# Chunked attention feeding a multiplicative FFN: transposes moved from DMA to 64x64 quadrants of the matrix engine

## Chip, core and metric

The kernel runs on one core of one Trainium2 chip. The metric is the device time of one execution in microseconds (us). Before the change it is about 313 us. A few runs are in a second, slower state (one of the four before, 318.63 us, is one): medians are over all runs, ratios over the fast ones alone. In a call of several kernels, all are timed in rounds beside the kernel before on the same chip. The engines are PE (matrix), DVE (vector), ACT (scalar), POOL (here, after setting up constants, it only issues loads), and SP (here it only issues DMAs).

## Reference

```python
# q, k, v: (8 batches, 8 heads, 576 tokens, 64); chunks of 64 tokens attend only to themselves
scores = 1/8 * q_c @ k_c.T          # per head and chunk, 64x64
attn   = softmax(scores)
x      = (attn @ v_c), heads side by side   # (4608 tokens, 512)
a = x @ w1; b = x @ w2              # 512 -> 1024
out = ((a * b) @ w3) @ w_out        # 1024 -> 1024 -> 512
```

The kernel multiplies w3 by w_out first (w3o), works in bfloat16, and walks over 36 units of 128 tokens (two chunks). In the kernel's matmuls the dimension that is summed over lies on partitions, so PE needs q and k with the head dimension on partitions, and x with its 512 features on partitions. What comes from memory, and what the value product gives, has tokens on partitions. Hence the transposes that this study is about: 8 blocks of 128x128 per unit for q and k, 4 for x.

## The kernel before

Loads are issued by POOL, which also casts float32 to bfloat16 on the way. After the first four units (the head, where PE transposes), every transpose is a DMA from SBUF to SBUF, issued by SP:

```python
def load(dst, src):
    return inorder(nc.gpsimd.dma_start(dst, src))
def turn(dst, src):
    return inorder(nc.sync.dma_start_transpose(dst, src))

def turn_qk(b, g0, g1):              # several 128x512 groups of one batch at a time
    turn(qkT_tile(b)[:, g0:g1]..., qk_t[b][:, g0:g1, :]...)
def turn_x(u):
    turn(xt[:, :, u * UT:(u + 1) * UT], xn_t.pop(u))

def do_S(u):    # 16 matmuls of 64x64, one per head and chunk, spread over four quadrants of the array; exp on ACT
def do_PV(u):   # 16 matmuls of 64x65 (the 65th column sums the weights); reciprocal, product on DVE -> xn
def PV_step(u):
    do_PV(u)
    turn_x(u)
# [cut] steady part, for each of four steps n of a tile t of 512 tokens:
place(0, lambda u=u: S_step(u + 1)); place(0, lambda u=u: PV_step(u))
do_ab(t, 2 * n); do_ab(t, 2 * n + 1); do_o(t - 1, n)
```

The softmax here doesn't subtract the row's maximum and nothing guards it: scores larger than these inputs give would overflow.

Of the kernel before, what the change touches and what calls it, by code (L numbers as in the profile page):

```python
# [11 lines left out]
def kernel(  # L12
# [54 lines left out]
    def turn(dst, src):  # L67

        return inorder(nc.sync.dma_start_transpose(dst, src))  # L69

# [14 lines left out]
    NP = S // UT  # L85
    G = 2 * NP + 1
    qk_t, qkT_t = {}, {}

    def rows(src, b, t0, n):
        return src[b, :, t0:t0 + n, :].rearrange("h p d -> p h d")  # L90

    def load_qk(b, i):
        if b not in qk_t:
            qk_t[b] = io.tile([P, G, DM], bf, tag="qk", bufs=3, name="qk")
        if i < NP:
            for t, src in enumerate((q, k)):
                load(qk_t[b][:, 2 * i + t, :].rearrange("p (h d) -> p h d", d=D),
                     rows(src, b, i * UT, UT))
        else:
            for p0, src in ((0, q), (CH, k)):  # L100
                load(qk_t[b][p0:p0 + CH, 2 * NP, :].rearrange("p (h d) -> p h d", d=D),
                     rows(src, b, NP * UT, CH))

    def load_batch(b):
        for i in range(NP + 1):
            load_qk(b, i)
# [9 lines left out]
    def qkT_tile(b):  # L116
        if b not in qkT_t:
            qkT_t[b] = io.tile([P, G, NHP, P], bf, tag="qkT", name="qkT")
        return qkT_t[b]

    def turn_qk(b, g0, g1):
        turn(qkT_tile(b)[:, g0:g1].rearrange("p g n t -> p (g n) t"),
             qk_t[b][:, g0:g1, :].rearrange("p g m -> p (g m)"))

    def pe_turn_qk(b, g):

        tp = ps.tile([P, NHP, P], bf, tag="m", bufs=4, name="qktp")
        for n in range(NHP):
            tr(tp[:, n, :], qk_t[b][:, g, n * P:(n + 1) * P], ident[:])
        nc.vector.tensor_copy(qkT_tile(b)[:, g], tp[:])  # L130

    def at(b, c, n, isk):
        i, o = divmod(c, 2)
        if i < NP:
            return qkT_t[b][:, 2 * i + isk, n, o * CH:(o + 1) * CH]
        return qkT_t[b][:, 2 * NP, n, isk * CH:(isk + 1) * CH]
# [3 lines left out]
    def chunk_at(u, ci):  # L140
        return divmod(2 * u + ci, NCH)

    NM = NHP // 2
    e_t, xn_t = {}, {}

    def do_S(u):
        sp = ps.tile([P, 2, 512], f32, tag="s", name="sp")
        sv = sp[:, :, 0:NHP * CH].rearrange("p r (m c q) -> p r m c q", m=NM, c=2)
        for ci in range(2):
            b, c = chunk_at(u, ci)  # L150
            for m in range(NM):
                for t in range(2):
                    for r in range(2):
                        h = slice(r * CH, (r + 1) * CH)
                        mm(sv[t * CH:(t + 1) * CH, r, m, ci, :],
                           lhsT=at(b, c, 2 * t + m, 1)[h], rhs=at(b, c, 2 * t + m, 0)[h],
                           start=True, stop=True)
        e = asb.tile([P, 2, NM, 2, CH], bf, tag="e", name="e")
        nc.scalar.activation(e[:].rearrange("p r m c q -> p r (m c q)"), sp[:, :, 0:NHP * CH],  # L159
                             Exp, scale=scale, bias=0.0)  # L160
        e_t[u] = e

    def do_PV(u):
        xp = ps.tile([P, 2, 512], f32, tag="x", name="xp")
        e = e_t.pop(u)
        W = D + 1
        for m in range(NM):
            for r in range(2):
                for ci in range(2):
                    b, c = chunk_at(u, ci)  # L170
                    for t in range(2):
                        h = slice(t * CH, (t + 1) * CH)
                        n = 2 * m + r
                        mm(xp[ci * CH:(ci + 1) * CH, t, n * W:(n + 1) * W],
                           lhsT=e[h, r, m, ci, :], rhs=vbuf[b % NV][h, n, c, 0:W],
                           start=True, stop=True)
        xv = xp[:, :, 0:NHP * W].rearrange("p t (n w) -> p t n w", w=W)
        rc = asb.tile([P, 2, NHP, 1], f32, tag="rc", name="rc")
        nc.vector.reciprocal(rc[:], xv[:, :, :, D:D + 1])  # L179
        xn = asb.tile([P, 2, NHP, D], bf, tag="xn", bufs=3, name="xn")  # L180
        nc.vector.tensor_mul(xn[:], xv[:, :, :, 0:D], rc.to_broadcast([P, 2, NHP, D]))  # L181
        xn_t[u] = xn[:].rearrange("p t n d -> p (t n d)")

    def turn_x(u):
        turn(xt[:, :, u * UT:(u + 1) * UT], xn_t.pop(u))

    def pe_turn_x(u):
        xn = xn_t.pop(u)
        tp = ps.tile([P, NHP, P], bf, tag="m", bufs=4, name="xtp")
        for n in range(NHP):  # L190
            tr(tp[:, n, :], xn[:, n * P:(n + 1) * P], ident[:])
        nc.vector.tensor_copy(xt[:, :, u * UT:(u + 1) * UT], tp[:])
# [12 lines left out]
    def do_a(t, j, tag="a_sb", bufs=2):  # L205
        n = tiles[t][1]
        a_ps = ps.tile([P, TT], f32, tag="m", bufs=4, name="a_ps")
        mm_ab(w1, a_ps, t, j)
        a_t[j] = msb.tile([P, TT], f32, tag=tag, bufs=bufs, name="a_sb")
        nc.scalar.copy(a_t[j][:, 0:n], a_ps[:, 0:n])  # L210
# [13 lines left out]
    def do_o(t, n):  # L224
        o_ps = ps.tile([P, DM], f32, tag="m", bufs=4, name="o_ps")
        for ki in range(FO):
            mm(o_ps[:], lhsT=ab_t[t][:, ki, n * P:(n + 1) * P],
               rhs=w3o[:, ki, :], start=(ki == 0), stop=(ki == FO - 1))
        o_sb = msb.tile([P, DM], f32, tag="o_sb", name="o_sb")
        nc.scalar.copy(o_sb[:], o_ps[:])  # L230
        r0 = tiles[t][0] + n * P
        inorder(nc.scalar.dma_start(out[r0:r0 + P, :], o_sb[:]))
# [24 lines left out]
    load_w(wo, moe_w_out, 0, DM)  # L257
# [4 lines left out]
    load_w3(0, 1)  # L262
    load_w3(1, 2)
    load_qk(0, 0)
    load_qk(0, 1)
    load_w3(2, 3)
    load_v(0)
    load_w3(3, 4)
    load_qk(0, 2)
    load_qk(0, 3)  # L270
# [6 lines left out]
    load_qk(0, 4)  # L277
    load_qk(1, 0)
    load_qk(1, 1)
    load_v(1)  # L280
    for i in range(2, NP + 1):
        load_qk(1, i)
    load_batch(2)
    load_v(2)



    pieces = ((0, 4), (4, 8), (8, 9))

    def S_step(u):  # L290
        do_S(u)
        for ci in range(2):
            b, c = chunk_at(u, ci)
            if b == 0:
                continue
            if c == 0 and b + 2 < B:
                load_batch(b + 2)
            if b + 1 < B:
                if b > 1 and c in (2, 4, 6):
                    turn_qk(b + 1, *pieces[c // 2 - 1])  # L300
                if b == 1 and c == 7:
                    for p in pieces:
                        turn_qk(2, *p)

    def PV_step(u):
        do_PV(u)
        turn_x(u)
        b = (2 * u + 2) // NCH
        if b != (2 * u) // NCH and b + 2 < B:
            load_v(b + 2)  # L310

    def pe_turn_unit(i):
        pe_turn_qk(0, 2 * i)
        pe_turn_qk(0, 2 * i + 1)
# [4 lines left out]
    pe_turn_unit(0)  # L319
    pe_turn_unit(1)  # L320
    do_w3o(1)
    do_w3T(2)
    do_S(0)
    do_w3o(2)
    do_S(1)
    do_PV(0)
    do_w3T(3)
    do_w3o(3)
    do_PV(1)
    pe_turn_unit(2)  # L330
    pe_turn_unit(3)
    pe_turn_x(0)
    do_w3T(4)
    do_S(2)
    do_w3T(5)
    do_w3o(4)
    pe_turn_x(1)
    do_S(3)
    do_PV(2)
    do_w3T(6)  # L340
    do_w3o(5)
    do_PV(3)
    pe_turn_x(2)
    do_w3T(7)
    do_w3o(6)
    pe_turn_x(3)
    do_w3o(7)

# [3 lines left out]
    def place(d, *what):  # L352
        units.setdefault(len(fill) + d, []).extend(what)

    for j in range(FO):
        fill.append(lambda j=j: do_a(0, j, "a0", FO))
    for j in range(FO):
        fill.append(lambda j=j: do_b(0, j))
    place(-2, lambda: (turn_qk(0, 8, 9), turn_qk(1, 0, 2), turn_qk(1, 2, 4)))
    place(0, lambda: S_step(4), lambda: turn_qk(1, 4, 6))  # L360
    place(1, lambda: S_step(5))
    place(2, lambda: PV_step(4))
    place(3, lambda: PV_step(5), lambda: turn_qk(1, 6, 8), lambda: turn_qk(1, 8, 9))
    for n in range(UPT):
        fill.append(lambda n=n: do_o(0, n))
    place(0, lambda: S_step(6))
    place(2, lambda: S_step(7))
    place(3, lambda: PV_step(6))
    place(5, lambda: PV_step(7))
    for j in range(FO):  # L370
        fill.append(lambda j=j: do_ab(1, j))
    place(0, lambda: S_step(8))
    us = list(range(8, NU))
    for t in range(2, len(tiles)):
        no = tiles[t - 1][1] // P if t > 1 else 0
        for n in range(4):
            if us:
                u = us.pop(0)
                if u + 1 < NU:
                    place(0, lambda u=u: S_step(u + 1))  # L380
                place(0, lambda u=u: PV_step(u))
            fill.append(lambda t=t, j=2 * n: do_ab(t, j))
            fill.append(lambda t=t, j=2 * n + 1: do_ab(t, j))
            if n < no:
                fill.append(lambda t=t, n=n: do_o(t - 1, n))
# [36 lines left out]
```

## Time and profile before

| | before |
|---|---|
| time, median of 4 runs | 313.65 us (312.12 to 318.63) |
| span of the profiled run | 311.3 us |
| first a matmul (end of the head) | 40.0 us |
| period of one step where PE has no holes | 5.66 us |

The page of the kernel before: the busy times; three rows of the 40 time slices in tenths (PE busy, the clock that PE was granted, DMA busy); the chain of work that ended last, by engine and by line.

```profile
span 311.3 us, 5443 instructions
PE 240.8 (77%) x2256; PEld 117.6 (38%) x2256; DVE 92.2 (30%) x175; ACT 89.4 (29%) x161; POOL 93.8 (30%) x113
...
PE   0497999909319604993999229989999999999995
...
PEclk9999999967958955999699859997999999999999
DMA  6999999999999999999999997992275322311013
...
PE 68%; DMA 22%; issue 4%; DVE 3%; POOL 1%; SPq 1%; ACT 0%; DVEq 0%; POOLq 0%
```

PE has holes (0 to 4 tenths) until slice 24, about 187 us, a last short one in slice 27, at 209 us, and none later. In most holes or just after them the mean granted clock of a slice falls to 5 to 8 tenths, and DMA is nearly full until they end. All waits of PE on transposes in this trace (what PE waited for: us in total, times, longest us):

```profile
PE a_ps L59 <- DMA xt<-xn: 18.3, 3, 11.0
PE sp L59 <- DMA qkT<-qk: 17.2, 3, 11.5
PE a_ps L59 <- issue: 16.9, 2, 11.0
```

The two waits put down to "issue" end at 148.6 and 184.5 us, each 0.1 us after a transpose of x has landed; so x accounts for 35.2 us, q and k for 17.2. The next view, cut from two windows, shows one hole, in order of time (start us, duration us, engine, instruction, and in brackets the engine's idle time before it and what ended it):

```profile
103.47 7.29 SPq L69 DMA_TRANSPOSE qkT<-qk  x1
103.94 0.30 PE L59 MATMUL xp<-vbuf_82,e 64*64 64x65 bf16 x16
104.56 0.69 DVE L181 TENSOR_TENSOR xn<-xp,rc 128x512 bf16<-128x512 f32 x1
...
109.65 0.42 PE L59 MATMUL xp<-vbuf_82,e 64*64 64x65 bf16 x16
...
110.85 1.49 SPq L69 DMA_TRANSPOSE xt<-xn  x1
...
112.45 1.27 SPq L69 DMA_TRANSPOSE qkT<-qk  x1
113.81 2.90 SPq L69 DMA_TRANSPOSE xt<-xn  x2
...
121.04 1.89 PE L59 MATMUL a_ps<-xt,w_74 128*128 128x512 bf16 x4 [10.98 <-DMA xt<-xn]
```

Counting the transposes of x in order (32, one per unit from unit 4 on), the one that PE waits for is that of unit 11, the last of its tile. PE did the values of this unit at 103.94, and x was ready at 105.3. (The values at 109.65 are those of the next tile's first unit.) But SP issues transposes one after another: one of q and k held it for 7.29 us, then x of unit 10 and another of q and k came first. The transpose was issued at 113.81 and landed at 121.0, and PE stood for 10.98 us. So of 15.7 us from ready to landed, 8.6 were the queue and 7.2 the transfer. Units 10 and 19 also waited 7.8 and 6.8 us in the queue, the other units of that time 0 to 4.3 us; up to 187 us all took 6.7 to 9.8 us to land. The four matmuls after one hole take 1.89 us, against 1.04 in the undisturbed step below. Granted clock by window of 10 us (the columns are the window, its length, then busy us and count of each engine, clock, DMA share, GB/s):

```profile
60.00:70.00 10.00, 2.85 (x42) 1.35 (x41) 0.90 (x2) 1.67 (x3) 4.91 (x7) 0.72 1.72 163
110.00:120.00 10.00, 0.07 (x7) 0.00 (x0) 0.90 (x2) 0.49 (x1) 3.90 (x5) 0.50 1.70 157
220.00:230.00 10.00, 10.00 (x108) 4.58 (x107) 4.13 (x8) 3.78 (x7) 0.00 (x0) 1.00 0.51 107
```

And where nothing disturbs it, one step of the kernel before, PE only (start us, duration us, engine, instruction):

```profile
246.09 0.30 PE L59 MATMUL xp<-vbuf_80,e 64*64 64x65 bf16 x16
246.32 1.04 PE L59 MATMUL a_ps<-xt,w_74 128*128 128x512 bf16 x4
247.20 1.03 PE L59 MATMUL b_ps<-xt,w_75 128*128 128x512 bf16 x4
...
249.79 1.89 PE L59 MATMUL o_ps<-w3o,ab 128*128 128x512 bf16 x8
251.61 0.32 PE L59 MATMUL sp<-qkT 64*64 64x64 bf16 x16
```

Printed durations of PE overlap (246.32 + 1.04 is later than 247.20); read starts. A group of four 512-column matmuls takes 0.865 us, so eight take 1.73 (what the next start comes later, 1.82, is counted to the scores), and the FFN part of a step is 4 x 0.865 + 1.73 = 5.19 us, and scores with values take the other 0.47 us of 5.66.

### The profile page before, as it was taken

Reading aid. Unit: us, or ns where it says so; the run is one execution under the profiler, and the core shown is the slowest. Engines: PE = TensorE matmul, PEld = TensorE weight load, DVE = VectorE, ACT = ScalarE, POOL = GpSimd, SP = SyncE. Lnnn points to the kernel's source line nnn. Section 1 sums busy time; section 2 is a strip of 40 time slices with the busy share of each in tenths; the row PEclk is TensorE's granted clock in tenths of the full one; section 3 lists DMA queues with packets and bytes.
Section 4 is the critical chain, followed back from the end, with each engine's and each line's share of the span. In section 5 each row is a group of like instructions: output and inputs, shape, how many; then the busy total and the mean of one; then the engine's idle time right before and its main releaser. Section 6 shows DMA issues by size and latency. Waiting matters only on the chain.

```text
span 311.3 us, 5443 instructions
## 1 busy us (share of the span) xinstructions
PE 240.8 (77%) x2256; PEld 117.6 (38%) x2256; DVE 92.2 (30%) x175; ACT 89.4 (29%) x161; POOL 93.8 (30%) x113
## 2 busy tenths in 40 slices
PE   0497999909319604993999229989999999999995
PEld 0345544406316401441344114433444444444442
DVE  0126506203304410342143203341443434332210
ACT  1022251223203400341144103341434334423332
POOL 8655372934643126452782110200000000000000
PEclk9999999967958955999699859997999999999999
DMA  6999999999999999999999997992275322311013
GB/s 93 184 170 200 207 163 141 153 167 188 145 151 158 160 166 156 141 179 158 155 155 165 162 153 89 148 178 59 86 149 124 95 59 58 96 53 67 34 67 136
DMA packets 172552, 41.77 MB, mean 134 GB/s; under 512 B 163824, under 2 KB 166896, under 8 KB 172528
## 3 DMA queue, kind: packets, MB, share of 16 engines
q0 software_dynamic: 116400, 19.41, 84.2%
q1 hardware_dynamic: 50944, 12.59, 32.0%
q10 hardware_dynamic: 5184, 9.44, 9.1%
q8 instruction: 17, 0.28, 0.4%
q14 instruction: 7, 0.06, 0.0%
HBM read 38.80 MB, written 9.44 MB: 155 GB/s over the span
## 4 chain that ended last, share of the span: by engine, by line
PE 68%; DMA 22%; issue 4%; DVE 3%; POOL 1%; SPq 1%; ACT 0%; DVEq 0%; POOLq 0%
PE a_ps L59 21%; PE b_ps L59 19%; PE o_ps L59 18%; DMA xt<-xn 16%; PE wp L59 5%; DMA qkT<-qk 4%; DMA w_76<-in_moe_w_dram 3%; PE sp L59 2%; PE xp L59 2%; DVE xn L181 1%; PE w3tp L62 1%; DVE w3T L241 1%; DVE qkT L130 1%; SPq L69 1%; DVE ab L218 0%
## 5 line engine op out<-in xcount | busy, mean ns | idle before, releaser
L59 PE MATMUL a_ps<-xt,w_74 128*128 128x512 bf16 (+1 forms) x320 | 80.9, 383 | 35.2 <-DMA xt<-xn 18.3
L218 DVE TENSOR_TENSOR ab<-a_sb,b_ps 128x512 bf16<-128x512 f32 (+1 forms) x80 | 50.7, 634 | 126.9 <-PE b_ps L59 126.6
L59 PE MATMUL b_ps<-xt,w_75 128*128 128x512 bf16 (+1 forms) x320 | 78.8, 375 | 0.0
L210 ACT COPY a_sb<-a_ps 128x512 f32<-128x512 f32 (+1 forms) x80 | 43.4, 543 | 90.9 <-PE a_ps L59 89.6
L59 PE MATMUL o_ps<-w3o,ab 128*128 128x512 bf16 x288 | 67.4, 380 | 0.0
L59 PEld LDWEIGHTS <-w_74 128*128 128x128 bf16 x320 | 30.4, 103 | 65.6 <-issue 25.7
L65 POOL DMA_DIRECT2D qk<-in_k_dram x40 | 34.1, 853 | 42.6 <-DMA qk<-in_k_dram 17.9
L59 PEld LDWEIGHTS <-w_75 128*128 128x128 bf16 x320 | 32.7, 102 | 34.5 <-issue 5.1
L65 POOL DMA_DIRECT2D qk<-in_q_dram x40 | 34.1, 852 | 28.0 <-DMA qk<-in_q_dram 11.5
L230 ACT COPY o_sb<-o_ps 128x512 f32<-128x512 f32 x36 | 21.1, 585 | 70.7 <-PE o_ps L59 62.4
L59 PEld LDWEIGHTS <-ab 128*128 128x128 bf16 x288 | 27.8, 98 | 32.8
L159 ACT ACTIVATE e<-sp 128x512 bf16<-128x512 f32 x36 | 21.6, 601 | 27.0 <-PE sp L59 26.9
L59 PE MATMUL sp<-qkT 64*64 64x64 bf16 x576 | 12.2, 202 | 17.2 <-DMA qkT<-qk 17.2
L181 DVE TENSOR_TENSOR xn<-xp,rc 128x512 bf16<-128x512 f32 x36 | 24.9, 691 | 1.9 <-DMA xt<-xn 0.8
L179 DVE RECIPROCAL rc<-xp 128x8 f32<-128x8 f32 x36 | 7.5, 207 | 58.6 <-PE xp L59 58.6
L59 PEld LDWEIGHTS <-qkT 64*64 64x64 bf16 x576 | 7.9, 110 | 30.7 <-DMA qkT<-qk 17.5
L59 PE MATMUL wp<-wo,w3T 128*128 128x512 bf16 x64 | 16.6, 407 | 1.9 <-DVE w3T L241 1.9
L62 PE MATMUL w3tp<-ident,w_76 128*128 128x128 bf16 x64 | 5.8, 243 | 12.4 <-DMA w_76<-in_moe_w_dram 11.8
L249 ACT CAST w3o<-wp 128x512 bf16<-128x512 f32 x8 | 4.7, 585 | 29.3 <-PE wp L59 29.3
L65 POOL DMA_DIRECT2D vbuf_81<-in_v_dram x6 | 6.9, 1149 | 19.0 <-PE xp L59 14.5
L59 PEld LDWEIGHTS <-w3T 128*128 128x128 bf16 x64 | 6.3, 104 | 9.0 <-DVE w3T L241 2.3
L241 DVE COPY w3T<-w3tp 128x1024 bf16<-128x1024 bf16 x8 | 5.4, 685 | 13.6 <-PE w3tp L62 13.6
(27 smaller groups left out, 57.8 us busy)
## 6 DMA issues: line engine op xcount, KB each, us to landing
out_dram<-o_sb ACTq DMA_DIRECT2D x36, 256.0 KB, 2.1
qk<-in_q_dram POOLq DMA_DIRECT2D x32, 128.0 KB, 12.6
qk<-in_k_dram POOLq DMA_DIRECT2D x32, 128.0 KB, 12.6
vbuf_80<-in_v_dram POOLq DMA_DIRECT2D x6, 288.0 KB, 14.2
vbuf_81<-in_v_dram POOLq DMA_DIRECT2D x6, 288.0 KB, 10.9
vbuf_82<-in_v_dram POOLq DMA_DIRECT2D x4, 288.0 KB, 15.3
wo<-in_moe_w_out_dram POOLq DMA_DIRECT2D x1, 1024.0 KB, 9.1
w_76<-in_moe_w_dram POOLq DMA_DIRECT2D x4, 256.0 KB, 9.4
```

What stands on the lines that cost most here:

```text
L59: return inorder(nc.tensor.matmul(*a, **kw))
L62: return inorder(nc.tensor.transpose(*a, **kw))
L65: return inorder(nc.gpsimd.dma_start(dst, src))
L69: return inorder(nc.sync.dma_start_transpose(dst, src))
L159: nc.scalar.activation(e[:].rearrange("p r m c q -> p r (m c q)"), sp[:, :, 0:NHP * CH], Exp, scale=scale, bias=0.0)
L179: nc.vector.reciprocal(rc[:], xv[:, :, :, D:D + 1])
L181: nc.vector.tensor_mul(xn[:], xv[:, :, :, 0:D], rc.to_broadcast([P, 2, NHP, D]))
L210: nc.scalar.copy(a_t[j][:, 0:n], a_ps[:, 0:n])
L218: nc.vector.tensor_mul(ab_t[t][:, j, 0:n], a_t.pop(j)[:, 0:n], b_ps[:, 0:n])
L230: nc.scalar.copy(o_sb[:], o_ps[:])
L241: nc.vector.tensor_copy(w3T_t[ko][:], tp[:])
L249: nc.scalar.copy(w3o[:, ko, :], wp[:])
```

## The change

Its intent: no DMA transposes at all. PE transposes q, k and x, in pieces of 64x64 that use the four quadrants of the array at once, as scores and values already do. One "slot" holds the transposes of x of unit s-3, those of q and k of unit s, the scores of unit s-1 and the values of unit s-2, so PE goes into the 64x64 mode once per unit. DVE copies the transposed blocks out of PSUM. Loads of q and k come per unit, ten units ahead. w3 is loaded before w_out; stores are issued by SP.

```diff
-    def turn(dst, src):
-        return inorder(nc.sync.dma_start_transpose(dst, src))
...
+    def do_slot(xu=None, tu=None, su=None, pu=None):
+        pa = ps.tile([P, 2, 512], f32, tag="pa", name="pa")   # scores and q,k transposes
+        pb = ps.tile([P, 2, 512], f32, tag="pb", name="pb")   # values and x transposes
+        if xu is not None:
+            for n in range(NHP):
+                for g in range(2):
+                    for r in range(2):
+                        tr(xv[half[g], r, n, :], xn[half[r], (2 * n + g) * D:(2 * n + g + 1) * D],
+                           ident[half[r], half[r]])
+        if tu is not None:
+            # the same for s in (q, k): 32 transposes of 64x64
+        if su is not None:
+            # 16 score matmuls, as before
+        if pu is not None:
+            # 16 value matmuls, as before
+        # exp on ACT; on DVE: qkT copy, xt copy, reciprocal, product
...
-    load_w(wo, moe_w_out, 0, DM)
...
+    load_w3(0, 1)
...
+    load_w3(1, 2)
+    load_w(wo, moe_w_out, 0, DM)
...
-        inorder(nc.scalar.dma_start(out[r0:r0 + P, :], o_sb[:]))
+        inorder(nc.sync.dma_start(out[r0:r0 + P, :], o_sb[:]))
```

More of the change, by code (lines that the diff above doesn't have):

```diff
@@ L82, with chunk_at, load_unit @@
         nc.vector.memset(vbuf[i][:, :, :, D:D + 1], 1.0)
-    NP = S // UT
-    G = 2 * NP + 1
-    qk_t, qkT_t = {}, {}
-    def rows(src, b, t0, n):
-        return src[b, :, t0:t0 + n, :].rearrange("h p d -> p h d")
-    def load_qk(b, i):
-        if b not in qk_t:
-            qk_t[b] = io.tile([P, G, DM], bf, tag="qk", bufs=3, name="qk")
-        if i < NP:
-            for t, src in enumerate((q, k)):
-                load(qk_t[b][:, 2 * i + t, :].rearrange("p (h d) -> p h d", d=D),
-                     rows(src, b, i * UT, UT))
-        else:
-            for p0, src in ((0, q), (CH, k)):
-                load(qk_t[b][p0:p0 + CH, 2 * NP, :].rearrange("p (h d) -> p h d", d=D),
-                     rows(src, b, NP * UT, CH))
-    def load_batch(b):
-        for i in range(NP + 1):
-            load_qk(b, i)
+    def chunk_at(u, ci):
+        return divmod(2 * u + ci, NCH)
+    NRAW = 10
+    qk_t = {}
+    def load_unit(u):
+        qk_t[u] = io.tile([P, 2, DM], bf, tag="qk", bufs=NRAW, name="qk")
+        (b0, c0), (b1, c1) = chunk_at(u, 0), chunk_at(u, 1)
+        parts = [(0, P, b0, c0)] if b0 == b1 else [(0, CH, b0, c0), (CH, P, b1, c1)]
+        for t, src in enumerate((q, k)):
+            for p0, p1, b, c in parts:
+                load(qk_t[u][p0:p1, t, :].rearrange("p (h d) -> p h d", d=D),
+                     src[b, :, c * CH:c * CH + p1 - p0, :].rearrange("h p d -> p h d"))
     def load_v(b):
@@ L114, in load_w @@
         load(dst[:, :, n0:n1], ap.rearrange("(ko p) n -> p ko n", p=P)[:, :, n0:n1])
-    def qkT_tile(b):
-        if b not in qkT_t:
-            qkT_t[b] = io.tile([P, G, NHP, P], bf, tag="qkT", name="qkT")
-        return qkT_t[b]
-    def turn_qk(b, g0, g1):
-        turn(qkT_tile(b)[:, g0:g1].rearrange("p g n t -> p (g n) t"),
-             qk_t[b][:, g0:g1, :].rearrange("p g m -> p (g m)"))
-    def pe_turn_qk(b, g):
-        tp = ps.tile([P, NHP, P], bf, tag="m", bufs=4, name="qktp")
-        for n in range(NHP):
-            tr(tp[:, n, :], qk_t[b][:, g, n * P:(n + 1) * P], ident[:])
-        nc.vector.tensor_copy(qkT_tile(b)[:, g], tp[:])
@@ L132, in at @@
-    def at(b, c, n, isk):
-        i, o = divmod(c, 2)
-        if i < NP:
-            return qkT_t[b][:, 2 * i + isk, n, o * CH:(o + 1) * CH]
-        return qkT_t[b][:, 2 * NP, n, isk * CH:(isk + 1) * CH]
-    def chunk_at(u, ci):
-        return divmod(2 * u + ci, NCH)
-    NM = NHP // 2
-    e_t, xn_t = {}, {}
-    def do_S(u):
-        sp = ps.tile([P, 2, 512], f32, tag="s", name="sp")
-        sv = sp[:, :, 0:NHP * CH].rearrange("p r (m c q) -> p r m c q", m=NM, c=2)
-        for ci in range(2):
-            b, c = chunk_at(u, ci)
-            for m in range(NM):
-                for t in range(2):
-                    for r in range(2):
-                        h = slice(r * CH, (r + 1) * CH)
-                        mm(sv[t * CH:(t + 1) * CH, r, m, ci, :],
-                           lhsT=at(b, c, 2 * t + m, 1)[h], rhs=at(b, c, 2 * t + m, 0)[h],
-                           start=True, stop=True)
-        e = asb.tile([P, 2, NM, 2, CH], bf, tag="e", name="e")
-        nc.scalar.activation(e[:].rearrange("p r m c q -> p r (m c q)"), sp[:, :, 0:NHP * CH],
-                             Exp, scale=scale, bias=0.0)
-        e_t[u] = e
@@ L163, in do_PV @@
-    def do_PV(u):
-        xp = ps.tile([P, 2, 512], f32, tag="x", name="xp")
-        e = e_t.pop(u)
-        W = D + 1
-        for m in range(NM):
-            for r in range(2):
-                for ci in range(2):
-                    b, c = chunk_at(u, ci)
-                    for t in range(2):
-                        h = slice(t * CH, (t + 1) * CH)
-                        n = 2 * m + r
-                        mm(xp[ci * CH:(ci + 1) * CH, t, n * W:(n + 1) * W],
-                           lhsT=e[h, r, m, ci, :], rhs=vbuf[b % NV][h, n, c, 0:W],
-                           start=True, stop=True)
-        xv = xp[:, :, 0:NHP * W].rearrange("p t (n w) -> p t n w", w=W)
-        rc = asb.tile([P, 2, NHP, 1], f32, tag="rc", name="rc")
-        nc.vector.reciprocal(rc[:], xv[:, :, :, D:D + 1])
-        xn = asb.tile([P, 2, NHP, D], bf, tag="xn", bufs=3, name="xn")
-        nc.vector.tensor_mul(xn[:], xv[:, :, :, 0:D], rc.to_broadcast([P, 2, NHP, D]))
-        xn_t[u] = xn[:].rearrange("p t n d -> p (t n d)")
@@ L184, in turn_x @@
-    def turn_x(u):
-        turn(xt[:, :, u * UT:(u + 1) * UT], xn_t.pop(u))
-    def pe_turn_x(u):
-        xn = xn_t.pop(u)
-        tp = ps.tile([P, NHP, P], bf, tag="m", bufs=4, name="xtp")
-        for n in range(NHP):
-            tr(tp[:, n, :], xn[:, n * P:(n + 1) * P], ident[:])
-        nc.vector.tensor_copy(xt[:, :, u * UT:(u + 1) * UT], tp[:])
+    NM = NHP // 2
+    HW = NHP * CH
+    W = D + 1
+    half = [slice(0, CH), slice(CH, P)]
+    qkT_t, e_t, xn_t = {}, {}, {}
+    def do_slot(xu=None, tu=None, su=None, pu=None):
+        if tu is not None or su is not None:
+            pa = ps.tile([P, 2, 512], f32, tag="pa", name="pa")
+        if xu is not None or pu is not None:
+            pb = ps.tile([P, 2, 512], f32, tag="pb", name="pb")
+        if xu is not None:
+            xn = xn_t.pop(xu)
+            xv = pb[:, :, 512 - NHP * CH // 2:512].bitcast(bf).rearrange("p r (n t) -> p r n t", t=CH)
+            for n in range(NHP):
[4 more added lines that the diff above has]
+        if tu is not None:
+            qk = qk_t.pop(tu)
+            tv = pa[:, :, HW:512].bitcast(bf).rearrange("p r (s n t) -> p r s n t", s=2, t=CH)
+            for s in range(2):
+                for n in range(NHP):
+                    for g in range(2):
+                        for r in range(2):
+                            tr(tv[half[g], r, s, n, :],
+                               qk[half[r], s, (2 * n + g) * D:(2 * n + g + 1) * D],
+                               ident[half[r], half[r]])
+        if su is not None:
+            qkT = qkT_t.pop(su)
+            sv = pa[:, :, 0:HW].rearrange("p r (m c q) -> p r m c q", m=NM, c=2)
+            for ci in range(2):
+                for m in range(NM):
+                    for t in range(2):
+                        for r in range(2):
+                            mm(sv[half[t], r, m, ci, :], lhsT=qkT[half[r], ci, 1, 2 * t + m, :],
+                               rhs=qkT[half[r], ci, 0, 2 * t + m, :], start=True, stop=True)
+        if pu is not None:
+            e = e_t.pop(pu)
+            for m in range(NM):
+                for r in range(2):
+                    for ci in range(2):
+                        b, c = chunk_at(pu, ci)
+                        for t in range(2):
+                            n = 2 * m + r
+                            mm(pb[half[ci], t, n * W:(n + 1) * W], lhsT=e[half[t], r, m, ci, :],
+                               rhs=vbuf[b % NV][half[t], n, c, 0:W], start=True, stop=True)
+        if su is not None:
+            e = asb.tile([P, 2, NM, 2, CH], bf, tag="e", name="e")
+            nc.scalar.activation(e[:].rearrange("p r m c q -> p r (m c q)"), pa[:, :, 0:HW],
+                                 Exp, scale=scale, bias=0.0)
+            e_t[su] = e
+        if tu is not None:
+            qkT_t[tu] = asb.tile([P, 2, 2, NHP, CH], bf, tag="qkT", bufs=3, name="qkT")
+            nc.vector.tensor_copy(qkT_t[tu][:].rearrange("p r s n t -> p r (s n t)"),
+                                  tv.rearrange("p r s n t -> p r (s n t)"))
+        if xu is not None:
+            nc.vector.tensor_copy(
+                xt[:, :, xu * UT:(xu + 1) * UT].rearrange("p n (r t) -> p r n t", r=2), xv)
+        if pu is not None:
+            pv = pb[:, :, 0:NHP * W].rearrange("p t (n w) -> p t n w", w=W)
+            rc = asb.tile([P, 2, NHP, 1], f32, tag="rc", name="rc")
+            nc.vector.reciprocal(rc[:], pv[:, :, :, D:D + 1])
+            xn = asb.tile([P, 2, NHP, D], bf, tag="xn", name="xn")
+            nc.vector.tensor_mul(xn[:], pv[:, :, :, 0:D], rc.to_broadcast([P, 2, NHP, D]))
+            xn_t[pu] = xn[:].rearrange("p t n d -> p (t n d)")
@@ L203, in mm_ab, with do_a @@
                start=(ki == 0), stop=(ki == KO - 1))
-    def do_a(t, j, tag="a_sb", bufs=2):
+    def do_a(t, j):
         n = tiles[t][1]
@@ L208, in do_a @@
         mm_ab(w1, a_ps, t, j)
-        a_t[j] = msb.tile([P, TT], f32, tag=tag, bufs=bufs, name="a_sb")
+        a_t[j] = msb.tile([P, TT], f32, tag="a_sb", bufs=FO, name="a_sb")
         nc.scalar.copy(a_t[j][:, 0:n], a_ps[:, 0:n])
@@ L255, in load_w3, with load_to, slot @@
         load(w3[:, k0:k1, :], w3v[:, k0:k1, :])
-    load_w(wo, moe_w_out, 0, DM)
+    loaded = [0]
+    def load_to(u):
+        while loaded[0] <= min(u, NU - 1):
+            load_unit(loaded[0])
+            loaded[0] += 1
+    def slot(s):
+        do_slot(*(u if 0 <= u < NU else None for u in (s - 3, s, s - 1, s - 2)))
+    load_w3(0, 1)
     inorder(nc.gpsimd.memset(ident[:], 0.0))
@@ L261 @@
         fill=1.0, base=0, pattern=[[-1, P]], channel_multiplier=1))
-    load_w3(0, 1)
     load_w3(1, 2)
-    load_qk(0, 0)
-    load_qk(0, 1)
+    load_w(wo, moe_w_out, 0, DM)
+    load_to(1)
     load_w3(2, 3)
+    load_w3(3, 4)
     load_v(0)
-    load_w3(3, 4)
-    load_qk(0, 2)
-    load_qk(0, 3)
+    load_to(3)
     load_w3(4, 6)
@@ L276 @@
             load_w(w, ap, n0, n0 + HF)
-    load_qk(0, 4)
-    load_qk(1, 0)
-    load_qk(1, 1)
+    load_to(5)
     load_v(1)
-    for i in range(2, NP + 1):
-        load_qk(1, i)
-    load_batch(2)
-    load_v(2)
-    pieces = ((0, 4), (4, 8), (8, 9))
-    def S_step(u):
-        do_S(u)
-        for ci in range(2):
-            b, c = chunk_at(u, ci)
-            if b == 0:
-                continue
-            if c == 0 and b + 2 < B:
-                load_batch(b + 2)
-            if b + 1 < B:
-                if b > 1 and c in (2, 4, 6):
-                    turn_qk(b + 1, *pieces[c // 2 - 1])
-                if b == 1 and c == 7:
-                    for p in pieces:
-                        turn_qk(2, *p)
-    def PV_step(u):
-        do_PV(u)
-        turn_x(u)
-        b = (2 * u + 2) // NCH
-        if b != (2 * u) // NCH and b + 2 < B:
-            load_v(b + 2)
-    def pe_turn_unit(i):
-        pe_turn_qk(0, 2 * i)
-        pe_turn_qk(0, 2 * i + 1)
+    load_to(9)
     do_w3T(0)
@@ L318 @@
     do_w3o(0)
-    pe_turn_unit(0)
-    pe_turn_unit(1)
+    do_slot(tu=0)
     do_w3o(1)
+    do_slot(tu=1, su=0)
     do_w3T(2)
-    do_S(0)
+    do_w3T(3)
     do_w3o(2)
-    do_S(1)
-    do_PV(0)
-    do_w3T(3)
     do_w3o(3)
-    do_PV(1)
-    pe_turn_unit(2)
-    pe_turn_unit(3)
-    pe_turn_x(0)
+    do_slot(tu=2, su=1, pu=0)
     do_w3T(4)
-    do_S(2)
+    do_slot(xu=0, tu=3, su=2, pu=1)
     do_w3T(5)
     do_w3o(4)
-    pe_turn_x(1)
-    do_S(3)
-    do_PV(2)
+    do_slot(xu=1, su=3, pu=2)
@@ L340, with place, run @@
     do_w3T(6)
     do_w3o(5)
-    do_PV(3)
-    pe_turn_x(2)
+    do_slot(xu=2, pu=3)
     do_w3T(7)
     do_w3o(6)
-    pe_turn_x(3)
+    do_slot(xu=3)
     do_w3o(7)
+    load_v(2)
+    load_to(13)
     fill, units = [], {}
-    def place(d, *what):
-        units.setdefault(len(fill) + d, []).extend(what)
+    def place(d, f, *a, **kw):
+        def run():
+            f(*a, **kw)
+            if "tu" in kw:
+                load_to(kw["tu"] + NRAW)
+        units.setdefault(len(fill) + d, []).append(run)
@@ L355, with place_slot @@
+    def place_slot(d, s):
+        place(d, slot, s)
+        place(d, load_to, s + NRAW)
+        for b in range(B - 3):
+            if (NCH * b + NCH - 1) // 2 == s - 2:
+                place(d, load_v, b + 3)
     for j in range(FO):
-        fill.append(lambda j=j: do_a(0, j, "a0", FO))
+        fill.append(lambda j=j: do_a(0, j))
+    place(4, do_slot, tu=4)
+    place(6, do_slot, tu=5, su=4)
     for j in range(FO):
         fill.append(lambda j=j: do_b(0, j))
-    place(-2, lambda: (turn_qk(0, 8, 9), turn_qk(1, 0, 2), turn_qk(1, 2, 4)))
@@ L360 @@
-    place(0, lambda: S_step(4), lambda: turn_qk(1, 4, 6))
-    place(1, lambda: S_step(5))
-    place(2, lambda: PV_step(4))
-    place(3, lambda: PV_step(5), lambda: turn_qk(1, 6, 8), lambda: turn_qk(1, 8, 9))
+    place(0, do_slot, su=5)
+    place(1, do_slot, pu=4)
+    place(1, load_v, 3)
+    place(2, do_slot, pu=5, xu=4, tu=6)
+    place(3, do_slot, xu=5, su=6)
     for n in range(UPT):
         fill.append(lambda n=n: do_o(0, n))
-    place(0, lambda: S_step(6))
-    place(2, lambda: S_step(7))
@@ L368 @@
-    place(3, lambda: PV_step(6))
-    place(5, lambda: PV_step(7))
+    place(1, do_slot, tu=7, pu=6)
+    place(3, do_slot, xu=6, su=7)
+    place(5, do_slot, tu=8, pu=7)
+    place(7, do_slot, xu=7, tu=9, su=8)
     for j in range(FO):
         fill.append(lambda j=j: do_ab(1, j))
-    place(0, lambda: S_step(8))
-    us = list(range(8, NU))
-    for t in range(2, len(tiles)):
-        no = tiles[t - 1][1] // P if t > 1 else 0
-        for n in range(4):
-            if us:
-                u = us.pop(0)
-                if u + 1 < NU:
-                    place(0, lambda u=u: S_step(u + 1))
-                place(0, lambda u=u: PV_step(u))
+    place(0, do_slot, tu=10, su=9, pu=8)
@@ new lines @@
+    place(0, load_v, 4)
+    place(2, do_slot, xu=8, tu=11, su=10, pu=9)
+    place(4, do_slot, xu=9, su=11, pu=10)
+    place(6, do_slot, xu=10, pu=11)
+    place(8, do_slot, xu=11)
+    for j in range(FO):
+        fill.append(lambda j=j: do_ab(2, j))
+    for n in range(2):
+        fill.append(lambda n=n: do_o(1, n))
+    place(0, do_slot, tu=12)
+    place(1, do_slot, tu=13, su=12)
+    place(2, do_slot, tu=14, su=13, pu=12)
+    for i, d in enumerate((3, 5, 7, 8)):
+        place_slot(d, 15 + i)
@@ L382 @@
+    for n in range(UPT):
+        fill.append(lambda j=2 * n: do_ab(3, j))
+        fill.append(lambda j=2 * n + 1: do_ab(3, j))
+        if n < 2:
+            fill.append(lambda n=n: do_o(2, n))
+    s = 19
+    for t in range(4, len(tiles)):
+        for n in range(UPT):
+            if s < NU + 3:
+                place_slot(0, s)
+                s += 1
             fill.append(lambda t=t, j=2 * n: do_ab(t, j))
             fill.append(lambda t=t, j=2 * n + 1: do_ab(t, j))
-            if n < no:
-                fill.append(lambda t=t, n=n: do_o(t - 1, n))
+            fill.append(lambda t=t, n=n: do_o(t - 1, n))
```

## The prediction

> **What bounds the kernel now.** The page gives a span of 311.3 us, PE busy 240.8. The chain of waits puts 15.6% on DMA transposes of x (xt<-xn), 3.8% on those of q and k, and 4.3% on "issue", which follows them: 74 us. In order of time these are holes of PE of 5 to 20 us at 61, 80, 102, 112, 137, 166 and 205 us; after 210 us, when the loads have ended, there is none. One transpose of x takes 6.9 us to land (DMA list) and shares the 16 engines with the q, k, v loads (110,592 packets of 128 bytes). Around the holes the granted clock falls to 0.5 to 0.8 (windows). So two things are lost: waits for transposes, and slow matmuls after them.
>
> **Taken away.** All 56 DMA transposes, hence those holes and most of the lost clock. Where only loads run, about 1,200 small packets per us land, the rate at which POOL issues them (0.87 us for 1,024): a unit's q, k, v take 2.3 us against 6 us of PE work, so loads won't bound the steady part.
>
> **Added.** Per unit 48 transposes of 64x64 on PE and two PSUM copies on DVE. The copies cost 0.69 us (like w3T, 128x1024) and 0.42 us (like xt<-xtp); with reciprocal 0.21, xn 0.69 and two ab products of 0.69, DVE works 3.4 us per unit, under PE's 6. ACT stays at 2.4. Copies hide, except where slots follow closely. On PE, the 64x64 matmuls of scores and values start in groups of four 32 ns apart when warm, 8 ns each; a whole S+PV step adds 0.47 us to 5.19 (period 5.66 in the steady part), about half of it entry and exit. This is below the 25 ns floor that the Trainium skill ("TensorE: Matmul & The Clock Gate", Back-to-back issue gap) states for small matmuls; the trace decides for bursts of 32. But a full slot has 80 pairs, 160 instructions, and the skill ("Advanced Engine Details and Errata", Engine Queue Depths) gives PE a queue of 64: beyond it the sequencer's rate may show, which no burst in this trace is long enough to tell. I take 14 ns per transpose: 0.67 us per unit, 21 us for the 32 units outside the head (at 8 ns 12 us, at 33 ns 50 us).
>
> **The sum.** Head, to the first a matmul: 40.2 us now; w3 comes first, so 37.5. FFN at full clock: 36 x 5.19 = 187. S and PV with entries 15. Transposes 21. More, smaller slots in the first tiles 2. Stalls: units 4 to 6 and v of batch 1 land just behind the weights at 41 to 49 us, 2 to 3; x transposes one fill after their xn, 3 to 4. Last store 4. Measured time over span 1.9. Total 273 us, 13% less.
>
> **Right or wrong, in the profile.** No DMA transposes; chain almost all PE; clock near 1.0 after 20 us; steady period 6.0 to 6.6 us; transposes 8 to 20 ns apart; PE idle under 20 us, mostly before 50 us; DVE busy near 130 us, POOL near 90.
>
> **What would make it wrong.** Transposes at 30 ns or more (slots of 2 us): 290 us. Waits on DVE or on single-buffered slot tiles in each slot: 285. Larger load stalls in the first 60 us: up to 10 more. Transposes at 8 ns and few stalls: 262.
>
> Chances: faster by over 2% 0.96, within 2% 0.03, slower 0.01. Range 260 to 289 us.

## More of the kernel before

A tile's first a matmul (do_ab) needs x of all four units of the tile. The last of them leaves do_PV only two pairs of products and one output block before that.

## The result

| | before | after |
|---|---|---|
| time, median of 4 runs | 313.65 us | 272.34 us (270.80 to 272.56) |
| ratio | | 0.8687, 95% interval 0.8634 to 0.8739 |
| span of the profiled run | 311.3 us | 270.6 us |
| first a matmul | 40.0 us | 42.9 us |
| undisturbed period | 5.66 us | 6.06 us |

A ratio is the mean time of one kernel's fast runs over that of the other's of the same rounds, so it isn't quite the ratio of the medians. The page of the changed kernel, the same lines:

```profile
span 270.6 us, 8708 instructions
PE 242.6 (90%) x3896; PEld 127.0 (47%) x3936; DVE 121.4 (45%) x235; ACT 91.2 (34%) x161; POOL 93.9 (35%) x113
...
PE   1198599999867999999999999999999999999994
...
PEclk9999799999999999999999999999999999999998
DMA  5999999999999999999997991211111111111223
...
PE 78%; DMA 10%; issue 3%; DVE 3%; POOL 2%; ACT 2%; ACTq 0%; POOLq 0%
```

The holes are gone, and with them the low clock: after 34 us it is full until PE has ended. DMA in the chain is now the start (weights) and the end (the last store), not transposes. What is left of holes lies at the start, in slice 5 and in slices 11 to 13. PE busy is the same to 1% although it does 1,680 more matmuls (by its weight loads, 3936 against 2256; some matmul records are missing): nearly all now run at the full clock. The steady step, PE only:

```profile
208.12 1.89 PE L59 MATMUL o_ps<-w3o,ab 128*128 128x512 bf16 x8
209.94 0.32 PE L62 MATMUL pb<-ident,xn 64*64 64x64 bf16 x16
210.09 0.43 PE L62 MATMUL pa<-ident,qk 64*64 64x64 bf16 x32
210.35 0.31 PE L59 MATMUL pa<-qkT 64*64 64x64 bf16 x16
210.47 0.32 PE L59 MATMUL pb<-vbuf_81,e 64*64 64x65 bf16 x16
210.72 1.04 PE L59 MATMUL a_ps<-xt,w_74 128*128 128x512 bf16 x3
```

The 32 transposes of q and k start at 210.09 and the scores follow at 210.35: 8 ns each. The step before began its slot at 203.88, so the period is 6.06 us, 0.40 more than before for 48 transposes. (Three matmuls of a are recorded instead of four: a few records are missing in a trace, and such a gap is no wait.) So in its last third the kernel before was faster per unit; the change wins by taking holes away, not by cheaper transposes.

Windows of the changed kernel at the same places, where the clock is 1.00:

```profile
60.00:70.00 10.00, 9.46 (x203) 5.65 (x205) 3.75 (x9) 3.39 (x7) 8.05 (x10) 1.00 2.18 196
110.00:120.00 10.00, 9.36 (x271) 5.16 (x272) 6.73 (x13) 4.22 (x8) 3.53 (x5) 1.00 1.86 142
220.00:230.00 10.00, 9.89 (x121) 4.68 (x122) 4.52 (x9) 3.60 (x7) 0.00 (x0) 1.00 0.13 49
```

Two waits are new. The first is in the head: PE waits for w_out and later for w3. (Its first matmul starts at 4.8 us; in the kernel before PE waited for w3 until 11.6 us, and then hardly for loads.)

```profile
13.73 3.57 PE L59 MATMUL wp<-wo,w3T 128*128 128x512 bf16 x8 [5.40 <-DMA wo<-in_moe_w_out_dram]
...
29.96 1.03 PE L62 MATMUL w3tp<-ident,w_76 128*128 128x128 bf16 x8 [3.25 <-DMA w_76<-in_moe_w_dram]
```

The second breaks a slot in the middle of a burst, with nothing that PE's instructions wait for ("issue"):

```profile
76.30 0.26 PE L59 MATMUL pa<-qkT 64*64 64x64 bf16 x7
78.17 0.28 PE L59 MATMUL pa<-qkT 64*64 64x64 bf16 x9 [1.60 <-issue]
```

The trace shows instruction fetches by DMA, in blocks of 16 KB on a queue of their own (queue 8: 31 packets, 17 in the kernel before). Their number goes with that of PE's instructions (7,832 and 4,512 in the pages, about 250 to 265 per block), so they are taken to be PE's. Laid against the breaks of the changed kernel, in us:

```
break starts   lasts   block lands at   PE goes on, after the landing
35.27          0.50    34.46            1.3
76.37          1.79    76.66            1.5
82.86          1.22    82.62            1.5
```

### The profile page after: what moved, and what is told of

The parts are those of the page before. It is cut to its first block, busy times and chain, and to the rows that moved or that the text cites. A ratio compares the mean times of both kernels' runs of the same rounds, so it can differ in the third digit from the quotient of the medians.

```text
span 270.6 us, 8708 instructions
## 1 busy us (share of the span) xinstructions
PE 242.6 (90%) x3896; PEld 127.0 (47%) x3936; DVE 121.4 (45%) x235; ACT 91.2 (34%) x161; POOL 93.9 (35%) x113
## 4 chain that ended last, share of the span: by engine, by line
PE 78%; DMA 10%; issue 3%; DVE 3%; POOL 2%; ACT 2%; ACTq 0%; POOLq 0%
PE a_ps L59 22%; PE b_ps L59 21%; PE o_ps L59 21%; DMA w_76<-in_moe_w_dram 4%; DMA wo<-in_moe_w_out_dram 4%; PE pa L62 3%; PE pb L62 3%; PE wp L59 3%; DMA out_dram<-o_sb 2%; PE pa L59 2%; PE pb L59 2%; DVE qkT L165 1%; POOL qk L65 1%; DVE xn L175 1%; PE w3tp L62 1%
## 5 line engine op out<-in xcount | busy, mean ns | idle before, releaser
L59 PE MATMUL b_ps<-xt,w_75 128*128 128x512 bf16 (+1 forms) x316 | 74.1, 357 | 0.8 <-ACT o_sb L214 0.3
L59 PE MATMUL a_ps<-xt,w_74 128*128 128x512 bf16 (+1 forms) x294 | 72.3, 357 | 1.6 <-issue 0.5
L194 ACT COPY a_sb<-a_ps 128x512 f32<-128x512 f32 (+1 forms) x80 | 43.4, 543 | 49.8 <-PE a_ps L59 47.4
L165 DVE COPY qkT<-pa 128x1024 bf16<-128x1024 bf16 x36 | 24.9, 691 | 20.1 <-PE pa L62 13.6
L168 DVE COPY xt<-pb 128x512 bf16<-128x512 bf16 x36 | 15.3, 424 | 40.8 <-PE pb L59 38.1
L160 ACT ACTIVATE e<-pa 128x512 bf16<-128x512 f32 x36 | 21.5, 598 | 28.9 <-PE pa L59 27.1
L175 DVE TENSOR_TENSOR xn<-pb,rc 128x512 bf16<-128x512 f32 x36 | 24.8, 690 | 1.0
L62 PE MATMUL pa<-ident,qk 64*64 64x64 bf16 x1152 | 16.2, 196 | 1.5 <-issue 1.0
L62 PEld LDWEIGHTS <-qk 64*64 64x64 bf16 x1152 | 12.9, 111 | 6.0 <-issue 5.8
L62 PEld LDWEIGHTS <-xn 64*64 64x64 bf16 x576 | 7.5, 108 | 16.0 <-issue 9.9
L62 PE MATMUL pb<-ident,xn 64*64 64x64 bf16 x576 | 11.6, 199 | 1.9 <-DVE xn L175 1.7
```

What stands on the lines that cost most here:

```text
L59: return inorder(nc.tensor.matmul(*a, **kw))
L62: return inorder(nc.tensor.transpose(*a, **kw))
L160: nc.scalar.activation(e[:].rearrange("p r m c q -> p r (m c q)"), pa[:, :, 0:HW], Exp, scale=scale, bias=0.0)
L165: nc.vector.tensor_copy(qkT_t[tu][:].rearrange("p r s n t -> p r (s n t)"), tv.rearrange("p r s n t -> p r (s n t)"))
L168: nc.vector.tensor_copy(xt[:, :, xu * UT:(xu + 1) * UT].rearrange("p n (r t) -> p r n t", r=2), xv)
L175: nc.vector.tensor_mul(xn[:], pv[:, :, :, 0:D], rc.to_broadcast([P, 2, NHP, D]))
```

## Experiments

Twelve runs; all gave correct results. Each time is the median of the run's rounds, with the ratio to the kernel before. Periods are the mean step over the undisturbed steps (10 in the kernel before, 14 or more in the others), from starts of output blocks in the trace.

### Where the gain comes from: one transpose at a time, in the old kernel

The theory was that both kinds of DMA transposes make holes. The rival was that the new order of loads and slots is what pays. These three runs keep the old kernel and move transposes to PE as full 128x128 blocks in steps of their own.

**b_pe_x**: only x on PE.

```diff
 def PV_step(u):
     do_PV(u)
-    turn_x(u)
...
+            place(0, lambda u=u: pe_turn_x(u))   # after the two products of the same step
```

> The kernel before, with the x transposes alone moved to PE as 12... four 128x128 transposes per unit (q and k stay on DMA). Theory (the DMA transposes are late because they share queue and engines, and both kinds make holes): the holes that end at xt<-xn go, those that end at qkT<-qk (about 18 us in the trace of before, at 62, 80 and 106 us) stay; PE gains 4 x 56 ns x 32 = 7 us of work; about 280 to 290 us. Rival (the gain of the change is its order of loads and slots): 305 us or more.

Measured: 279.75 us, ratio 0.888 (0.883 to 0.894), period 5.89 us. The holes at xt<-xn are gone. Those at qkT<-qk remain, but are 7.2 us and not the 17 to 18 of the kernel before:

```profile
PE sp L59 <- DMA qkT<-qk: 7.2, 4, 4.2
```

In the main as the theory expects, though the time is just under its range; that these holes shrank too was not expected, and no run shows why. The rival is out: loads and slots are the old ones.

**b_pe_qk**: only q and k on PE.

```diff
-                    turn_qk(b + 1, *pieces[c // 2 - 1])
...
+        turn_for(u + 1)     # pe_turn_qk of the groups that the next unit needs
```

> The kernel before, with the q and k transposes alone moved to PE (eight 128x128 per unit), x stays on DMA. Theory: the x transposes no longer stand behind long q, k transposes in the one queue, land in 3 to 5 us instead of 6.9, and only small holes at tile starts remain (10 us in all); PE gains 14 us of work; about 280 to 290 us. Rival (x transposes are slow because they share the 16 engines with the loads, whoever else is in their queue): landing stays near 7 us and the holes at xt<-xn stay, 300 us or more.

Measured: 295.26 us, ratio 0.937 (0.929 to 0.944). A miss: neither theory fits as written. The transposes of x, now alone in their queue, landed in

```profile
DMA to landing us min/median/max: 2.4/3.5/10.0
```

The same line for the kernel before has 2.4, 6.9 and 9.8. The median hides two stretches. While loads run, to 184 us, most took 4 to 7 us, the first two 10; after that 2.4 to 2.5 (2.4 to 4.0 in the kernel before, from 209 us on). And each was now issued within 0.03 us of its x being ready, where three had stood 6.8 to 8.6 us in the queue. So two things made x late: the queue, which this edit empties, and the transfer itself, which stays slow while loads run. (The edit also takes the transfers of q and k away; how much of the faster landing that brings, no run shows.) PE still waits 17.1 us for x in four holes, 9.3% of the chain: a tile's first product comes too soon after the last x.

**b_pe_both**: both, no DMA transposes.

```diff
 # the edits of b_pe_x and b_pe_qk together
```

> The kernel before, with no DMA transposes, all transposes as 128x128 on PE in separate steps between the matmuls, loads still by batch, no shared slots. Theory: nearly the whole gain comes from leaving the DMA transposes; steady period 5.66 + 12 x 0.056 = 6.33 us, time 273 to 282 us. Rival (quadrants and shared slots are what pays): 290 us or more, with waits of PE on DVE copies or PSUM buffers in each step.

Measured: 282.00 us, ratio 0.894 (0.887 to 0.900), at the upper edge of what was expected; the period is 6.58 us and not 6.33. The trace shows why: the full transposes of q and k stand between scores and values, so PE goes into the 64x64 mode twice in a step.

```profile
211.31 0.32 PE L59 MATMUL sp<-qkT 64*64 64x64 bf16 x16
211.56 0.62 PE L62 MATMUL qktp<-ident,qk 128*128 128x128 bf16 x8
212.11 0.32 PE L59 MATMUL xp<-vbuf,e 64*64 64x65 bf16 x16
```

There are nearly no holes, and still it is not faster than b_pe_x (the intervals overlap). Moving x to PE is worth 35 us (314.68 to 279.75). Moving q and k after that, as full blocks in steps of their own, costs about as much PE time (0.69 us per step) as it saves in holes and low clock.

### What the slots and quadrants are worth

Four runs, on the changed kernel.

**a_again**: no edit.

> The changed kernel itself, unedited, as the yardstick of this call: 271 to 273 us, steady period 6.06 us.

Measured: 272.71 us, ratio 0.868 (0.863 to 0.872), period 6.06.

**a_full**: full 128x128 transposes in the same slots.

```diff
-                for g in range(2):
-                    for r in range(2):
-                        tr(xv[half[g], r, n, :], xn[half[r], ...], ident[half[r], half[r]])
+                tr(xv[:, n // 2, n % 2, :], xn[:, n * P:(n + 1) * P], ident[:])
... # the same for q and k; scores and copies read the new layout
```

> The changed kernel with the 48 quadrant transposes per unit replaced by 12 full 128x128 ones in the same slots, everything else kept. Theory (the array is what a transpose costs: 48 x 8.3 = 0.40 us against 12 x 56 = 0.67 us): steady period 6.3 to 6.35 us, 4 to 9 us slower than the changed kernel. Rival (the saving of the quadrants is all in saved mode switches or lies off the critical path): the same time within 1 us. With 1,152 fewer pairs of instructions the pauses at 76 and 82 us of the changed kernel should go, if they are waits for instruction fetches.

Measured: 276.81 us, ratio 0.881 (0.877 to 0.885), period 6.33. The transposes in its steady step:

```profile
208.00 0.39 PE L62 MATMUL pb<-ident,xn 128*128 128x128 bf16 x4
208.22 0.61 PE L62 MATMUL pa<-ident,qk 128*128 128x128 bf16 x8
208.76 0.32 PE L59 MATMUL pa<-qkT 64*64 64x64 bf16 x16
```

Twelve take about 0.67 us against 0.40 for 48 quadrants. The breaks with "issue" at 76 and 82 us are gone, with 1,296 fewer pairs of instructions in the program (36 for each of 36 units; the expectation counted 32). Both as expected.

**a_split**: from unit 19 on, each slot cut in two.

```diff
-                place_slot(0, s)
+                # transposes of x, q, k before the first pair of products:
+                place(0, do_slot, only(s - 3), only(s))
+                # scores and values before the second pair:
+                place(1, do_slot, None, None, only(s - 1), only(s - 2))
```

> The changed kernel with each slot of the steady part (from unit 19 on) cut in two: transposes of x, q and k before the first pair of products, scores and values before the second. Theory (entry into and exit from the quadrant mode cost some 0.25 us a time): steady period 6.3 us, 4 to 6 us slower. Rival (sharing a slot saves nothing, a wait is hidden either way): within 1 us.

Measured: 277.04 us, ratio 0.881 (0.877 to 0.886), period 6.28: one more entry into the quadrant mode and exit from it costs 0.22 us.

```profile
207.50 0.43 PE L62 MATMUL pa<-ident,qk 64*64 64x64 bf16 x32
208.09 0.81 PE L59 MATMUL a_ps<-xt,w 128*128 128x512 bf16 x3 [0.16 <-issue]
...
209.69 0.32 PE L59 MATMUL pa<-qkT 64*64 64x64 bf16 x16
```

The Trainium skill ("TensorEngine Tiling (Array Packing)", Key Properties) says that changing the tiling mode drains the engine; 0.22 us is what such a pair of changes costs here.

These two close the sum between the periods of b_pe_both and of the changed kernel: 6.06 + 0.27 (full blocks) + 0.22 (a second entry) = 6.55, measured 6.58.

**a_twice**: every quadrant transpose done twice into the same place, so that a full slot has 128 pairs.

```diff
-            for n in range(NHP):
+            for n in [*range(NHP), *range(NHP)]:
...
-            for s in range(2):
+            for s in (0, 1, 0, 1):
```

> The changed kernel with every quadrant transpose done twice into the same place (correct result, 96 transposes per unit, 128 pairs per full slot). Theory (8.3 ns each, hidden by nothing): steady period 6.46 us, and 13 us plus a few us of longer instruction-fetch pauses on top, 285 to 290 us. Rival (a queue of 64 or a sequencer rate that shows only beyond some length of burst): the added 48 cost more than 15 ns each, period over 6.8 us, 295 us or more.

Measured: 296.00 us, ratio 0.944 (0.938 to 0.951). The time is over the range of the theory, and the rival named a time like this; but the period decides between them, and it is 6.46 us, 8.3 ns for each added transpose. Its steady slot:

```profile
238.74 0.44 PE L62 MATMUL pb<-ident,xn 64*64 64x64 bf16 x32
239.01 0.70 PE L62 MATMUL pa<-ident,qk 64*64 64x64 bf16 x64
239.53 0.32 PE L59 MATMUL pa<-qkT 64*64 64x64 bf16 x16
```

No sign of a queue of 64: 64 transposes go at the same 8 ns as 32. What grew is the breaks. Ten of over 0.7 us from 36 to 148 us sum to 12 us, each within 2 us after the start of a fetch, and PE goes on 1.2 to 1.5 us after the block has landed. That the breaks are waits for fetches is read from this timing and from a_full. In these kernels they grow with the number of fetched blocks (none with a_full's 20, three with 31 in the changed kernel, ten with 44 here); the number is not all, as the next section shows. They come where slots stand close together, or in stretches that also load; after 150 us there is none. The Trainium skill ("Runtime: NRT & Kernel Launch", Instruction fetch mechanics) has the fetch in 16 KiB blocks, as seen, but calls it mostly hidden; in these bursts it wasn't.

### Attempts to go below both kernels

**a_head**: the first loads in the order of the kernel before.

```diff
-    load_w3(0, 1)
+    load_w(wo, moe_w_out, 0, DM)
... # ident
+    load_w3(0, 1)
     load_w3(1, 2)
-    load_w(wo, moe_w_out, 0, DM)
     load_to(1)
     load_w3(2, 3)
+    load_v(0)
     load_w3(3, 4)
-    load_v(0)
```

> The changed kernel with the order of the first loads of the kernel before (w_out first, v of batch 0 before the fourth block of w3), nothing else. Theory (the changed order lets w_out land later, POOL's v load waits for it, and all loads behind are 3 us late): the first a matmul moves from 42.7 to about 40 us, the wait of 3.4 us for w3 at 27 us goes, 2 to 3 us faster, 269.5 to 270.5 us. Rival (PE is bound by its own work in the head, a wait is only moved): within 1 us of the changed kernel.

Measured: 271.84 us, ratio 0.862 (0.859 to 0.865), first a at 42.1 us. A miss: 0.9 us less than the yardstick (by the ratios 0.7%, 1.9 us, and their intervals overlap). It was run at another time. The wait for w3 at 27 us halves, but PE now waits 2 us for another block of w3 at 21 us, and a break of instruction fetch at 34 us is 1.4 us, against 0.5 at 35 us before. The order of w_out explains little of the late head.

**a_mix16**: as a_head, and q and k of units 16 to 35 transposed by DMA again, each asked for four units ahead; x stays in the slots, stores go to ACT.

```diff
+    def turn_unit(u):
+        qkT_t[u] = asb.tile([P, 2, NHP, P], bf, tag="qkTd", bufs=LEAD + 2, name="qkTd")
+        inorder(nc.sync.dma_start_transpose(..., qk_t.pop(u)...))
...
+        place(d, turn_to, s + LEAD)
```

> As a_head, and q and k of units 16 to 35 transposed by DMA again, four units ahead, with x still on PE in the slots and the stores issued by ACT. Theory (DMA transposes harm only where PE waits for them at once, as for x; q and k can be asked for 20 us early): steady period 5.79 us, no holes, 5 us faster than a_head, 263 to 266 us. Rival (any DMA transpose slows loads, or is itself slowed, so that PE waits): holes ending at qkT<-qk, 268 us or more.

Measured: 268.61 us, ratio 0.851 (0.848 to 0.855), period 5.79 as expected. There is no hole at qkT. The transposes took 4 to 13 us to land, and no matmul waited for one, since they are asked for 20 us early.

```profile
DMA to landing us min/median/max: 3.9/8.2/12.6
```

The total missed its range: a_head, on which it stands, gave less, and a break of 1.9 us came at 107 us. (Its time is in the range of the rival, but the holes that the rival names are not there.) No run tests the move of the stores to ACT alone. This is the fastest version. The ratios to the kernel before put it 1.8% under the changed kernel (0.8514 over 0.8671). They were run at other times.

**a_mix10**: the same from unit 10, three units ahead.

```diff
-    U0, LEAD = 16, 4
+    U0, LEAD = 10, 3
```

> As a_mix16 but from unit 10 on, three units ahead. Fewer instructions in the dense slots take the fetch pauses at 76 and 82 us away (3 us) and 1.6 us of transposes: 259 to 263 us if the transposes land in time; but the loads of units 10 to 16 and these transposes meet at 60 to 90 us, where the kernel before had qkT holes: if they come late, 265 us or more.

Measured: 271.35 us (270.36 without the one slow run of six, which is left out of the ratio), ratio 0.857 (0.853 to 0.862). The time falls into the second case; it is 0.7% slower than a_mix16, with intervals that overlap. The trace shows a wait of 3.6 us for an output copy at 68 us, and breaks of 1.2 to 2.8 us at 80, 89 and 95 us; it does not tell which of these the transposes cause. The program has only 24 blocks to fetch, so the number of instructions doesn't explain breaks of this length.

**a_mix16_head**: a_mix16, with w3 loaded earlier and the head's steps reordered.

```diff
     load_to(1)
     load_w3(2, 3)
-    load_v(0)
     load_w3(3, 4)
-    load_to(3)
     load_w3(4, 6)
+    load_v(0)
+    load_to(3)
     load_w3(6, 8)
... # head: one w3 transpose, then the product of the one before, in turn
```

> As a_mix16, with w3 loaded before v and units 2 and 3, and the head's compute steps reordered so that no two transposes of w3 stand before the products that they feed. Theory (the head is bound by when the blocks of w3 land, not by PE): first a matmul at 39.5 to 40.5 us instead of 42.1, 266 to 267 us. Rival (PE-bound head, or what is saved there comes back as waits for units 2 to 5): first a matmul before 41 us but the time within 1 us of 268.6.

Measured: 271.09 us, ratio 0.862 (0.858 to 0.865), first a at 43.4 us. A miss: the saved wait came back as 3 us of waits for q and k of unit 2 at 25 to 28 us, and a break of 3.8 us came at 107 us. There PE stops at 106.6, the fetch of a block starts only at 107.8 and lands at 108.9, and PE goes on at 110.4: here the fetch itself was late, in a stretch where loads and transposes fill the DMA engines (DMA 9 tenths or more). Neither case came true as written. In the three orders tried the waits of the head moved from one load to another; I did not find the order that does better.

**a_same**: no edit, beside it.

> The changed kernel, unedited, beside it on the same chip: 272 to 273 us.

Measured: 272.74 us, ratio 0.867 (0.863 to 0.871).

## Why the prediction was right

The time was 272.34 us, predicted 273, and the main reason holds: the holes came from DMA transposes, and PE can do them in less. But two terms of the sum were off, one by 5.4 us up and one by 8.2 us down, and cancelled: that the total fits within 1 us is luck. Each measured term is from the profiled run.

| term | predicted, us | measured, us |
|---|---|---|
| head, to the first a matmul | 37.5 | 42.9 |
| FFN at full clock, 36 x 5.19 | 187 | 187 |
| scores and values with entries, 32 x 0.47 | 15 | 15 |
| 48 transposes for 32 units | 21 | 12.8 (32 x 0.40) |
| more slots, load stalls, x stalls | 7 to 9 | 9.1 (what is left) |
| last store | 4 | 3.8 |
| time over span | 1.9 | 1.8 |

- **Holes and clock: right.** With the same terms, the 311.3 us of before are a head of 40.0, FFN 187, scores and values 15, a last store of 3.8, single gaps of over 0.3 us after the head that sum to 54 us (from start to start, less the usual step), and a rest of 11.5 us, mostly matmuls at a low clock. The changed kernel has none of those gaps; b_pe_x shows that moving x alone brings 35 us. What the prediction left out is the queue: it has x late by its landing (6.9 us) alone, and up to 8.6 us were spent before the issue.
- **Transposes: too dear.** I took 14 ns out of doubt about a queue of 64 instructions, between the 8 ns that scores and values showed and 33 ns. The period gives 8.3 ns, and a_twice the same for 128 pairs. The number in the trace was right, also beyond its burst length.
- **Head: too short.** I took it as bound by PE, with a start earlier by w3. In the trace it stands on loads: PE starts at 4.8 us, then waits 1.4 us for w3, 5.4 us for w_out and 3.3 us for w3 again, 14.9 us with the start; in the kernel before it is 11.6 us to the first matmul and then less than 1 us.
- **Stalls: right in sum, wrong in kind.** There is no gap over 0.3 us at 41 to 49 us, so the loads of units 4 to 6 were in time. What is there: 3.0 us of instruction fetch, which I had not thought of, 3.3 us of transposes and copies waiting for DVE in the dense slots (predicted 3 to 4), and 0.5 us for an output copy. The other 2.3 us would be ten more slots than units at 0.22 us, an estimate from a_split.
- **DVE, POOL, clock: right in the main.** 121.4 and 93.9 us busy; clock 1.00 from 34 us on (20 was predicted; the wait for w3 at 27 us is followed by 3.4 us at 0.5). PE idle was 28 us and not under 20, for the head's sake.

## What to carry to other kernels

A DMA transpose made no matmul wait where it was asked for 20 us early (a_mix16), and cost much where its consumer came next (x, 35 us): look first at the one with the short lead, and at what stands before it in the same queue. Started earlier, beside more loads, the same trick brought less (a_mix10). Small matmuls and transposes on quadrants are cheap per piece (8 ns) when they share one entry into the mode (0.22 us), but they eat program at 160 instructions in less than a microsecond, and the breaks for fetches came where such slots stood close together or beside loads. A total that fits can hide two wrong terms: check each of them against the trace.

## What the Trainium skill lacked or had wrong

- "TensorE: Matmul & The Clock Gate" (Back-to-back issue gap) states a floor near 25 ns per small matmul, without saying how it counts on quadrants. Here 64x64 matmuls and transposes start in groups of four, one group every 32 ns: 8 ns each over a slot of 128 pairs, but no quadrant by itself starts faster than the floor.
- "TensorEngine Tiling (Array Packing)" (Key Properties) has the drain at a change of mode without its size: an extra entry and exit cost 0.22 us here.
- "Runtime: NRT & Kernel Launch" (Instruction fetch mechanics) calls block fetches mostly hidden. Here PE broke off for 0.5 to 1.8 us in the changed kernel, and went on 1.3 to 1.5 us after a block had landed; in a_mix16_head a break took 3.8 us.
- "Advanced Engine Details and Errata" (X-Bar Transpose) says that transpose DMAs are as fast as regular ones. It has no figure for what loads do to them: one 128 KB transpose of x landed in 2.4 us alone, and in 6.7 to 9.8 us in the kernel before up to 187 us, under the loads (mostly 4 to 7 us in b_pe_qk, with x alone in its queue).
